# Two pairs of PSUM tiles made into one ring of four, and loads of the second MLP laid between its products

## The chip, the core and the metric

The kernel runs on one core of one Trainium2 chip. Its engines are TensorE (PE, matrix products; PEld is its loading of weights), VectorE (DVE), ScalarE (ACT), GpSimd (POOL) and SyncE (SP, which here only issues DMA transfers). Products are written to PSUM, of which this program uses eight tiles ("banks" here) of 128 x 512 fp32 values; the other engines read them there. The metric is the device time of one launch in microseconds. Lower is better.

## The reference

```python
# x (8, 8, 512, 64), state (8, 8, 32, 64): B, H, S|Ns, D
scores  = x @ state^T / 8;  a  = softmax(scores);   xread = a @ state
scores2 = state @ x^T / 8;  a2 = softmax(scores2);  sread = a2 @ x
t = concat([xread, sread], axis=2)           # per batch and head, 544 rows
t = t.transpose(0, 2, 1, 3).reshape(4352, 512)
h = t @ moe_w_in;   g = max(h, 0) + alpha * min(h, 0);  t = g @ moe_w_out     # 512 -> 2048 -> 512
h = t @ moe2_w_in;  g = h - tanh(h);                    out = g @ moe2_w_out  # 512 -> 2048 -> 512
```

All data are fp32. The kernel carries each fp32 operand as a high and a low part and makes a product in three terms (`TERMS`: high by high, and the two mixed ones).

## The kernel before

**First MLP.** The 4352 tokens are nine blocks: 0 to 7 are the 512 `x` rows of a batch each, the last holds the 256 `state` rows. A *visit* (blk, f) works on one block and one of the 16 slices of 128 columns of the hidden layer:

- `emit_h` (L595) makes the *first product*: 12 matmuls (L605) into a PSUM tile `ps_h`, from the pool `ps_h`, which has two banks.
- `act_a` (L609) has ACT write `t = slope * h` (L612), DVE write `h = max(...)` in place in PSUM (L613), ACT write g's high part (L614); `act_b` (L617) has DVE write g's low part (L618). That last read gives the bank of `ps_h` back.
- `emit_o` (L623) adds the *previous* visit's g times `w_out` to the four accumulators `acc` (L633, 12 matmuls). They hold four banks for a whole block.

**Between the matmuls of the visits** a table of visits and places (`plan`) lays the next batch's attention and the products of its states, in short steps. These take their banks from the pool `ps_a`, two banks, by turns: transposes of x `ps_xt` (L460), scores `ps_s` (L494), transposed scores `ps_e` (L528), the read states `ps_r` (L558), `ps_w` (L583), state products' transposes `ps_st` (L361) and the products of a batch's states with `w_in`, `ps_p` (L410, `project_one`). Each is released by its last reader: `ps_p` by DVE L414 (its low part; ACT L413 writes the high one before), `ps_r` by DVE L568 (`wide`), `ps_xt` by ACT L465, `ps_st` and `ps_e` by ACT and DVE (`e2t` L530 among them). Early in the kernel DVE also splits raw weights into parts (`cm`, L115 to L120). The order of instructions is fixed on every engine; an engine works its own in that order.

**Second MLP.** It runs in five *tasks* (block pairs 0, 1, 2, the state rows B, pair 3) of four *octets* each. An octet (L810) makes 14 products of 6 matmuls (L820, `ps_m`), from the task's prepared x tiles and one *chunk* of combined weights (`ch`, seven parts of 512 KB, `load_chunk` L711). Its results are combined (`c` L826 by ACT and L837 by DVE, `t` L830 and L831) and stored to DRAM as `g` (L808, 256 KB each). A task's raw x, the *pair* `rx`, is four loads of 512 KB (`load_pair`, L722, L726). `bank()` (L798) hands out PSUM banks by turns from all three pools. After the tasks, `unit` (L965) makes the last products (L1001).

All these DMAs are issued by SP in the order of the program, and a store is issued behind the loads that stand before it. At the start of a task SP issues the pair of the next one, and in task 0 also the seven parts of chunk 2, before the task's first store. `octet` calls `between(n)` after its product n; there, short steps of a later preparation are made (`fill.go`).

Of the kernel before, what the change touches and what calls it, by code (L numbers as in the profile page):

```python
# [12 lines left out]
F32 = mybir.dt.float32  # L13
# [6 lines left out]
PSUM = bass.MemoryType.PSUM  # L20
DRAM = bass.MemoryType.DRAM

P = 128
# [12 lines left out]
def attention_and_two_mlps(ctx, tc, x, state, w1_in, w1_out, alpha, w2_in, w2_out, out):  # L36
    nc = tc.nc
    B, H, S, D = x.shape
# [18 lines left out]
    w_outs = tc.alloc_tile_pool(name="w_outs", bufs=NF // FQ)  # L57
    w_ins = tc.alloc_tile_pool(name="w_ins", bufs=NF // FQ, side="right")
    ps_acc = ctx.enter_context(tc.tile_pool(name="ps_acc", bufs=4, space=PSUM))
    ps_h = ctx.enter_context(tc.tile_pool(name="ps_h", bufs=2, space=PSUM))  # L60
    ps_a = ctx.enter_context(tc.tile_pool(name="ps_a", bufs=2, space=PSUM))
    dram = ctx.enter_context(tc.tile_pool(name="dram", bufs=1, space=DRAM))

    blocks = [(b, S) for b in range(B)] + [(B, NSB)]
    y_dram = [dram.tile([NCC, P, n], F32, name=f"y{b}") for b, n in blocks]
# [28 lines left out]
    def w_in(f, part):  # L94
        return WI[f // FQ][:, part].rearrange("p c (f m) -> p c f m", f=FQ)[:, :, f % FQ, :]
# [251 lines left out]
    def lead(b):  # L347
        return b if b % 2 or b == B - 1 else b - 1
# [244 lines left out]


    def emit_h(blk, n, f):  # L595
        ps = ps_h.tile([P, S], F32, tag="h", name="ps_h")
        if 0 < blk < B:
            col = slice(f % FQ * P, (f % FQ + 1) * P)
            pairs = [([PW[blk, f // FQ, g][i][:, col] for i in range(2)], X[0, blk, g]) for g in range(NG)]
        else:  # L600
            w = [WS[f][:, i] if blk else w_in(f, i) for i in range(2)]
            pairs = [([w[i][:, cc, :] for i in range(2)], X[0, blk, cc]) for cc in range(NCC)]
        for k, (w, xt) in enumerate(pairs):
            for m, (i, j) in enumerate(TERMS):
                nc.tensor.matmul(ps[:, :n], lhsT=w[i], rhs=xt[:, j, :n], start=(k == 0 and m == 0),  # L605
                                 stop=(k == len(pairs) - 1 and m == 2))
        return ps[:, :n]
# [94 lines left out]
    slots, small = Slots(), Slots()  # L702
# [8 lines left out]
    def load_chunk(o, i):  # L711

        t = slots.get([P, 2, 2, HW], F32R, f"ch{o}_{i}")
        nc.sync.dma_start(out=t.bitcast(F32), in_=wc_dram[0][o][i].rearrange("j p h c -> p j h c"))
        CH[o, i] = t
# [3 lines left out]

    RX, XT = {}, {}  # L720

    def load_pair(u):  # L722
        for k in range(2):
            for m in range(2):
                t = slots.get([P, 2, S], F32, f"rx{u}_{k}{m}")
                nc.sync.dma_start(out=t, in_=y_dram[2 * u + m][2 * k:2 * k + 2].rearrange("c p n -> p c n"))  # L726
                RX[u, k, m] = t

    def split_to(o, src):
        nc.scalar.copy(o[:, 0], src)  # L730
# [65 lines left out]
    turn = [0]  # L796

    def bank(shape=(P, S)):  # L798

        pool, tag = ((ps_a, "a"), (ps_a, "a"), *[(ps_acc, "acc")] * 4, (ps_h, "h"), (ps_h, "h"))[turn[0] % 8]  # L800
        turn[0] += 1
        return pool.tile(list(shape), F32, tag=tag, name="ps_m")

# [55 lines left out]
    def load_state_block():  # L859
        for k in range(2):  # L860
            XS["r", k] = slots.get([P, 2, NSB], F32, f"xsr{k}")
            nc.sync.dma_start(out=XS["r", k], in_=y_dram[B][2 * k:2 * k + 2].rearrange("c p n -> p c n"))
# [13 lines left out]
    def state_slices(j, between):  # L876


        ps = bank((P, 2, NSB))
        for m, pair in enumerate((((P1, "1"), (P2, "2")), ((P5, "1"), (P4, "d")))):  # L880
            for a, (i, x) in enumerate(pair):
                w = [chunk(j, i, p) for p in range(2)]
                for cc in range(2):
                    for k, (p, q) in enumerate(TERMS):
                        nc.tensor.matmul(ps[:, m], lhsT=w[p][:, cc], rhs=XS[x][:, q, cc],  # L885
                                         start=(a == cc == k == 0), stop=(a == cc == 1 and k == 2))
            between(m)
        t = small.get([P, 2, NSB], F32, f"ts{j}")
        nc.scalar.activation(t, ps, AF.Tanh)
        nc.vector.tensor_tensor(t, ps, t, op=ALU.subtract)  # L890
        for m in range(2):
            store_g(B, m, j, t[:, m])
        small.put(t)
# [4 lines left out]
    def load_weights(i):  # L898
        WP[i] = []
        for jj in range(NJ // 2):  # L900
            t = slots.get([P, 2, 2, HW], F32R, f"wp{i}_{jj}")
            nc.sync.dma_start(out=t.bitcast(F32), in_=wc_dram[1][jj][i].rearrange("r p h c -> p r h c"))
            WP[i].append(t)

    def load_g(blk, k):
        n = blocks[blk][1]
        for jj in range(NJ // 2):
            t = slots.get([P, 2, n], F32, f"gt{blk}_{k}_{jj}")
            nc.sync.dma_start(out=t, in_=g_dram[blk, k, jj].rearrange("r p n -> p r n"))
            GT[blk, k, jj] = t  # L910
# [151 lines left out]
    with tc.manual_schedule():  # L1062
# [5 lines left out]
        a = attention(0, 0)  # L1068
        c = attention(0, 1, spare=True)
# [22 lines left out]
        a = attention(1, 0)  # L1092
# [9 lines left out]
        for b in range(2, B):  # L1102
            for g in range(NG):
                i, f = (0, 0) if b == 2 else (b - 2, 6 + 7 * g) if b == lead(b) else (b - 2, 1 + g)
# [26 lines left out]
        for i, (blk, n) in enumerate(seq):  # L1131
            if i + 1 < B:
                timetable(i, a, attention(i + 1, 1))
                if i + 2 < B:
                    a = attention(i + 2, 0)
# [31 lines left out]
        def open_slots():  # L1167
            for _ in combined:
                pass
            late_pools[0].release()  # L1170
            freed.append(tc.alloc_tile_pool(name="slots_a", bufs=1, side="right", reuse_waits="tile"))
            slots.add(freed[0], "a", 16)
            load_pair(0)
            for i in range(7):
                load_chunk(0, i)
# [12 lines left out]
        for i, f in visits:  # L1188
            blk, n = seq[i]
# [26 lines left out]
        pool = tc.alloc_tile_pool(name="slots_b", bufs=1, reuse_waits="tile")  # L1216
# [6 lines left out]
        for i in range(7):  # L1223
            load_chunk(1, i)
        at_visit = 0
        for k, (u, os) in enumerate(tasks):
            coming = tasks[k + 1][0] if k + 1 < len(tasks) else None
            if coming is None:
                load_weights(P1)
                load_g(0, 0)  # L1230
                load_g(0, 1)
            elif coming == B:
                load_state_block()
                load_pair(3)
            elif u != B:
                load_pair(coming)
            if k == 0:
                for i in range(7):
                    load_chunk(2, i)
            for n_o, o in enumerate(os):  # L1240
                rest = visits[at_visit + 1:]
                following = next((v for v in rest if v > 1), None)

                def used(i):
                    if o not in rest or (o > 1 and following != o):
                        slots.put(CH.pop((o, i)))
                        if o > 1 and following is not None:
                            load_chunk(following, i)

                at_visit += 1  # L1250
                if u == B:
                    for j in (2 * o, 2 * o + 1):
                        state_slices(j, lambda m: fill.go(2))
                    for i in (P1, P2, P5, P4, P6, P3, P7):
                        used(i)
                    continue
                last = n_o == len(os) - 1

                def between(n):
                    if k == 0 and n_o == 0 and n < 5:  # L1260
                        fill.go(3)
                    if coming is None:
                        if n_o == 2 and n == 5:
                            fill.start(prepare_all())
                        if len(ST) < 4:
                            fill.go(1)
                        return
                    if n_o == 1 and n == 0:
                        if coming == B:
                            def both():  # L1270
                                yield from prepare_state_block()
                                yield from prepare_pair(3, 3)
                            fill.start(both())
                        else:
                            fill.start(prepare_pair(coming, coming))
                    if last or n % 2:
                        fill.go(1)

                octet(u, u, (2 * o, 2 * o + 1), between, last, used)
                if coming is None and n_o in (1, 2):  # L1280
                    load_weights((P5, P6)[n_o - 1])
            if u == B:
                for name in "12d":
                    slots.put(XS.pop(name))
            if coming is not None and coming != B:
                fill.finish()
# [40 lines left out]
```

## Time and profile before

| | |
|---|---|
| median of 3 runs | 1509.73 us (1509.43 to 1513.57) |
| the profiled execution | 1510.44 us, span of its work 1508.6 us |
| mean granted TensorE clock | 0.982 |
| PE busy | 1422.1 us, 94% of the span, 8188 matmuls |
| DVE / ACT / POOL busy | 991.6 (66%) / 729.7 (48%) / 532.1 (35%) us |
| 29 to 814 us | first products of the first MLP (L605) and their visits |
| 815 to 1158 us | products of the second MLP's octets (L820) |
| 1158 to 1508 us | its last products (L1001) |

Times in the trace are us from the start of the span. PE is busy nearly all the time, so what counts is its idle gaps, and in which stage another engine sets the pace. A row of a *timeline* gives start, duration, engine, line, operation, tile out<-in, how many instructions it joins, and in brackets the idle time of the engine just before and whose work ended it.

### The profile page before, as it was taken

The numbers are of one execution on the slowest core, as the hardware profiler recorded it, in microseconds if no ns is written. First come the engines' busy times: TensorE is split into PE (matmuls) and PEld (weight loads), VectorE is DVE, ScalarE is ACT, GpSimd is POOL, SyncE is SP. The second block draws the span as 40 slices with busy tenths as digits, with TensorE's granted clock in tenths as the row PEclk, the third lists the DMA queues.
The fourth block names the chain that finished last, engine by engine and source line by source line (L and its number), as shares of the span: only waits on it lengthen the run. The fifth ranks groups of instructions, "written<-read, shape, count | busy, mean of one in ns | idle before, by whom it ended". The sixth has DMA issues, their size and how long they took to land. (4 is left out here: it accounts for less than half of the span.)

```text
span 1508.6 us, 22873 instructions
## 1 busy us (share of the span) xinstructions
PE 1422.1 (94%) x8188; PEld 1192.1 (79%) x8188; DVE 991.6 (66%) x1430; ACT 729.7 (48%) x1322; POOL 532.1 (35%) x414
## 2 busy tenths in 40 slices
PE   5868899999899999999999899999999999999998
PEld 2656687677677677778887787887988999999998
DVE  6879855556577667676345555646347798788874
ACT  3656543444565555555334444545345444444443
POOL 2545400000254444445200222212016486666662
PEclk9998999999999999999999999999999999999999
DMA  5458628795688587749864666272795834444321
GB/s 150 137 163 253 206 80 286 268 300 129 188 213 238 156 247 225 239 158 298 237 209 151 253 202 247 103 272 105 276 346 205 324 133 141 133 141 140 133 85 36
DMA packets 230979, 294.41 MB, mean 195 GB/s; under 512 B 57809, under 2 KB 133585, under 8 KB 229841
## 3 DMA queue, kind: packets, MB, share of 16 engines
q1 hardware_dynamic: 228608, 292.39, 60.2%
q8 instruction: 64, 1.05, 0.3%
q10 hardware_dynamic: 2256, 0.56, 0.2%
q14 instruction: 51, 0.41, 0.1%
HBM read 170.73 MB, written 122.16 MB: 194 GB/s over the span
## 5 line engine op out<-in xcount | busy, mean ns | idle before, releaser
L633 PE MATMUL acc<-g,wo 128*128 128x512 f32 (+1 forms) x1728 | 416.2, 388 | 20.8 <-ACT g L614 11.8
L633 PEld LDWEIGHTS acc<-g,wo 128*128 128x128 f32 x1728 | 312.2, 191 | 104.0 <-ACT g L614 16.6
L1001 PE MATMUL ps_m<-wp,s 128*128 128x256 f32 x2856 | 343.5, 283 | 2.1 <-ACT e L984 2.0
L1001 PEld LDWEIGHTS ps_m<-wp,s 128*128 128x128 f32 x2856 | 342.5, 191 | 3.2 <-ACT e L984 2.2
L820 PE MATMUL ps_m<-x,ch 128*128 128x512 f32 x1344 | 312.7, 394 | 8.6 <-DVE c L837 4.5
L820 PEld LDWEIGHTS ps_m<-x,ch 128*128 128x128 f32 x1344 | 251.7, 188 | 69.0 <-DVE c L837 6.5
L946 DVE TENSOR_TENSOR s<-gt,s 128x512 fp32r<-128x512 f32 (+1 forms) x216 | 220.5, 1072 | 45.4 <-ACT s L962 44.4
L613 DVE SCALAR_TENSOR_TENSOR ps_h<-ps_h,sign,t 128x512 f32<-128x512 f32 (+1 forms) x144 | 104.7, 727 | 144.9 <-ACT t L612 144.4
L614 ACT ACTIVATE g<-ps_h,sign 128x512 fp32r<-128x512 f32 (+1 forms) x144 | 95.8, 666 | 160.5 <-DVE ps_h L613 160.5
L962 ACT CAST s<-gt 128x512 fp32r<-128x512 f32 (+1 forms) x216 | 120.3, 597 | 90.9 <-PE ps_m L1001 37.5
L605 PE MATMUL ps_h<-x,pw 128*128 128x512 f32 x624 | 162.7, 396 | 0.9 <-DMA pw<-pw 0.9
L618 DVE SCALAR_TENSOR_TENSOR g<-ps_h,sign,g 128x512 fp32r<-128x512 f32 (+1 forms) x144 | 102.6, 713 | 62.1 <-ACT g L614 58.9
L612 ACT ACTIVATE t<-ps_h,slope 128x512 f32<-128x512 f32 (+1 forms) x144 | 95.7, 664 | 88.3 <-PE ps_h L605 88.0
L605 PEld LDWEIGHTS ps_h<-x,pw 128*128 128x128 f32 x624 | 114.4, 188 | 26.1 <-issue 1.3
L237 POOL TENSOR_TENSOR c_q<-c_m,c_q 128x512 int32<-128x512 int32 x32 | 42.2, 1319 | 262.3 <-ACT c_q L124 213.0
L831 POOL TENSOR_TENSOR t<-c,t 128x512 f32<-128x512 f32 x32 | 41.7, 1303 | 252.1 <-ACT t L830 239.9
L830 ACT ACTIVATE t<-c 128x512 f32<-128x512 f32 x96 | 60.5, 632 | 123.2 <-DVE c L837 110.3
L837 DVE TENSOR_TENSOR c<-ps_m,c 128x512 f32<-128x512 f32 x96 | 64.7, 685 | 58.9 <-PE ps_m L820 43.2
L264 POOL TENSOR_TENSOR c_o<-c_q,c_o 128x512 fp32r<-128x512 f32 (+1 forms) x48 | 54.4, 1134 | 109.6 <-ACT c_o L262 109.6
L831 DVE TENSOR_TENSOR t<-c,t 128x512 f32<-128x512 f32 x64 | 53.9, 843 | 46.6 <-ACT t L830 46.6
L928 POOL TENSOR_TENSOR s<-gt,gt 128x512 f32<-128x512 f32 (+1 forms) x36 | 53.5, 1492 | 83.2 <-DMA gt<-g 81.5
L167 POOL TENSOR_TENSOR cq<-cm,cq 128x512 int32<-128x512 int32 x32 | 42.0, 1313 | 95.7 <-DVE cm L120 60.5
(138 smaller groups left out, 1663.0 us busy)
## 6 DMA issues: line engine op xcount, KB each, us to landing
g<-t SPq DMA_DIRECT2D x128, 256.0 KB, 2.3
gt<-g SPq DMA_DIRECT2D x64, 512.0 KB, 4.9
wc<-c_o SPq DMA_DIRECT2D x112, 256.0 KB, 3.4
ch<-wc SPq DMA_DIRECT2D x56, 512.0 KB, 7.6
pw<-pw SPq DMA_DIRECT2D x104, 256.0 KB, 5.1
wp<-wc SPq DMA_DIRECT2D x28, 512.0 KB, 7.6
raw<-in_moe_w_in SPq DMA_DIRECT2D x16, 512.0 KB, 4.6
raw<-in_moe_w_out SPq DMA_DIRECT2D x16, 512.0 KB, 4.8
```

Of the source, the lines that this page charges most:

```text
L605: nc.tensor.matmul(ps[:, :n], lhsT=w[i], rhs=xt[:, j, :n], start=(k == 0 and m == 0), stop=(k == len(pairs) - 1 and m == 2))
L612: nc.scalar.mul(t, ph, slope[:, f:f + 1])
L613: nc.vector.scalar_tensor_tensor(ph, ph, sign[:, f:f + 1], t, op0=ALU.mult, op1=ALU.max)
L614: nc.scalar.mul(g[:, 0, :n], ph, sign[:, f:f + 1])
L618: nc.vector.scalar_tensor_tensor(g[:, 1, :n], ph, sign[:, f:f + 1], g[:, 0, :n].bitcast(F32), op0=ALU.mult, op1=ALU.subtract)
L633: nc.tensor.matmul(acc[t][:, :n], lhsT=w[i][:, t * P:(t + 1) * P], rhs=g[:, j, :n], start=(first and k == 0), stop=(last and k == 2))
L820: nc.tensor.matmul(b, lhsT=w[p][:, cc], rhs=XT[key, i][cc][:, q], start=(i not in GOES_ON and cc == k == 0), stop=(cc == 1 and k == 2), sk ...
L831: eng.tensor_tensor(t, h, t, op=ALU.subtract)
L837: nc.vector.tensor_tensor(h, ps[j, i], h, op=ALU.add)
L946: nc.vector.tensor_tensor(made[k - 1][:, 1], src, made[k - 1][:, 0].bitcast(F32), op=ALU.subtract)
L962: nc.scalar.copy(made[k][:, 0], source(blk, i, jj))
L1001: nc.tensor.matmul(dst[:, t * HW:(t + 1) * HW], lhsT=s[:, p, r, t * P:(t + 1) * P], rhs=w[:, q], start=first, stop=(jj == NJ // 2 - 1 and ...
```

## The change

The two pools of two banks become one pool of four, `ps_a`, which serves first products, attention and states' products alike; `bank()` takes four banks of it and then the four of `ps_acc`. `load_pair` gets a part of its own for each load. In the second MLP's tasks 0 and 1 the next pair's four loads, and in task 0 chunk 2's seven loads, are put in a list, and one is taken from it after every odd product of an octet.

```diff
-    ps_h = ctx.enter_context(tc.tile_pool(name="ps_h", bufs=2, space=PSUM))
-    ps_a = ctx.enter_context(tc.tile_pool(name="ps_a", bufs=2, space=PSUM))
+    ps_a = ctx.enter_context(tc.tile_pool(name="ps_a", bufs=4, space=PSUM))
...
     def emit_h(blk, n, f):
-        ps = ps_h.tile([P, S], F32, tag="h", name="ps_h")
+        ps = ps_a.tile([P, S], F32, tag="a", name="ps_h")
...
+    def load_pair_part(u, k, m):
+        t = slots.get([P, 2, S], F32, f"rx{u}_{k}{m}")
+        nc.sync.dma_start(out=t, in_=y_dram[2 * u + m][2 * k:2 * k + 2].rearrange("c p n -> p c n"))
+        RX[u, k, m] = t
...
     def bank(shape=(P, S)):
-        pool, tag = ((ps_a, "a"), (ps_a, "a"), *[(ps_acc, "acc")] * 4, (ps_h, "h"), (ps_h, "h"))[turn[0] % 8]
+        pool, tag = (*[(ps_a, "a")] * 4, *[(ps_acc, "acc")] * 4)[turn[0] % 8]
...
+        loads = deque()
         for k, (u, os) in enumerate(tasks):
...
             elif u != B:
-                load_pair(coming)
+                loads.extend(partial(load_pair_part, coming, h, m) for h in range(2) for m in range(2))
             if k == 0:
-                for i in range(7):
-                    load_chunk(2, i)
+                loads.extend(partial(load_chunk, 2, i) for i in range(7))
...
                 def between(n):
+                    if loads and n % 2:
+                        loads.popleft()()
```

The instructions of PE, DVE, ACT and POOL stay the same and in the same order; what changes there is what they wait for. On PE, at one place of the first MLP (about 82 to 98 us of the trace; names are tiles, and a wait names the engine waited for), it reads so before:

```order
L410 MATMUL ps_p_919<-wi0_342,snp_784 128x512 [waits DVE_49]
L410 MATMUL ps_p_919<-wi0_342,snp_784 128x512 x2
L633 MATMUL acc_518<-g_787,wo1_704 128x512 x3
L633 MATMUL acc_519<-g_787,wo1_704 128x512 x3
L633 MATMUL acc_520<-g_787,wo1_704 128x512 x3
L633 MATMUL acc_521<-g_787,wo1_704 128x512 x3
L410 MATMUL ps_p_939<-wi0_342,snp_784 128x512 [waits DVE_49]
L410 MATMUL ps_p_939<-wi0_342,snp_784 128x512 x2
L460 MATMUL ps_xt_947<-ident_90,xr1_1_405 128x128 [waits DMAHW1_49,DMAHW0_49,DVE_49]
L460 MATMUL ps_xt_947<-ident_90,xr1_1_405 128x128 x3
L605 MATMUL ps_h_966<-x0_0_0_350,wi1_666 128x512 [waits Activation_49]
```

and so in the changed kernel, where these line numbers are one less:

```order
L409 MATMUL ps_p_916<-wi0_339,snp_781 128x512 [waits PE_49]
L409 MATMUL ps_p_916<-wi0_339,snp_781 128x512 x2
L632 MATMUL acc_515<-g_784,wo1_701 128x512 x3
L632 MATMUL acc_516<-g_784,wo1_701 128x512 x3
L632 MATMUL acc_517<-g_784,wo1_701 128x512 x3
L632 MATMUL acc_518<-g_784,wo1_701 128x512 x3
L409 MATMUL ps_p_936<-wi0_339,snp_781 128x512 [waits DVE_49]
L409 MATMUL ps_p_936<-wi0_339,snp_781 128x512 x2
L459 MATMUL ps_xt_944<-ident_87,xr1_1_402 128x128 [waits DMAHW1_49,DMAHW0_49,DVE_49]
L459 MATMUL ps_xt_944<-ident_87,xr1_1_402 128x128 x3
L604 MATMUL ps_h_963<-x0_0_0_347,wi1_663 128x512 [waits DVE_49,Activation_49]
```

The first product `ps_h` of the last row now also waits for DVE: its bank is one of the four, and was the previous first product's, released by L618. The second `ps_p` and `ps_xt` wait on DVE in both, but for banks that were given back earlier: `ps_p` for the bank of the `ps_p` two before it in place of that of `ps_r`, `ps_xt` for that of `ps_r` in place of that of the `ps_p` before it.

On SP, at the start of the second MLP (`rx` the next pair, `ch2` chunk 2, `g` a store of results), it reads so before:

```order
L714 DMA ch1_6_7725<-wc0_1_98 128x2x512
L726 DMA rx1_00_7727<-y2_83 128x2x512
L726 DMA rx1_01_7729<-y3_84 128x2x512
L726 DMA rx1_10_7731<-y2_83 128x2x512
L726 DMA rx1_11_7733<-y3_84 128x2x512
L714 DMA ch2_0_7735<-wc0_2_99 128x2x512
L714 DMA ch2_1_7737<-wc0_2_99 128x2x512
L714 DMA ch2_2_7739<-wc0_2_99 128x2x512
L714 DMA ch2_3_7741<-wc0_2_99 128x2x512
L714 DMA ch2_4_7743<-wc0_2_99 128x2x512
L714 DMA ch2_5_7745<-wc0_2_99 128x2x512
L714 DMA ch2_6_7747<-wc0_2_99 128x2x512
```

and in the changed kernel:

```order
L713 DMA ch1_6_7722<-wc0_1_95 128x2x512
L723 DMA rx1_00_7751<-y2_80 128x2x512
L723 DMA rx1_01_7793<-y3_81 128x2x512
L810 DMA g1_0_0_146<-t0_01_7811 128x512
L723 DMA rx1_10_7815<-y2_80 128x2x512
L810 DMA g1_0_0_146<-t1_01_7832 128x512
L723 DMA rx1_11_7836<-y3_81 128x2x512
L810 DMA g1_1_0_150<-t0_11_7845 128x512
L810 DMA g0_0_0_138<-t0_00_7857 128x512
L713 DMA ch2_0_7861<-wc0_2_96 128x2x512
L810 DMA g1_1_0_150<-t1_11_7870 128x512
L810 DMA g0_0_0_138<-t1_00_7882 128x512
```

The eleven loads, which stood in one row ahead of the first store, now stand between the stores of the first two octets.

## Rows read from the trace of the kernel before

**Rows 1.** Windows by stage: busy time of each engine, granted clock (1 is full), DMA.
```profile
44.00:165.00 121.00, 95.95 (x496) 71.43 (x495) 104.24 (x163) 76.23 (x141) 63.04 (x48) 0.90 0.64 193
165.00:708.00 543.00, 517.74 (x2652) 398.48 (x2651) 346.55 (x593) 275.49 (x498) 159.66 (x153) 0.99 0.70 212
814.00:860.00 46.00, 40.70 (x175) 32.20 (x174) 28.77 (x40) 21.84 (x40) 9.07 (x5) 1.00 0.79 293
```
**Rows 2.** Waits of PE, 44 to 165 us: us in total, times, longest.
```profile
PE ps_xt L460 <- DVE wi L414: 4.1, 1, 4.1
PE ps_p L410 <- DVE wi L414: 3.2, 1, 3.2
PE ps_st L361 <- ACT e2t L530: 2.2, 1, 2.2
```
**Rows 3.** The timeline of PE, 77 to 98 us.
```profile
78.83 3.05 PE L605 MATMUL ps_h<-x,wi 128*128 128x512 f32 x12
92.38 1.11 PE L460 MATMUL ps_xt<-ident,xr 128*128 128x128 f32 x4 [4.13 <-DVE wi L414]
93.14 4.66 PE L605 MATMUL ps_h<-x,wi 128*128 128x512 f32 x12
```
**Rows 4.** The timeline of DVE, 53 to 100 us.
```profile
53.70 0.76 DVE L613 SCALAR_TENSOR_TENSOR ps_h<-ps_h,sign,t 128x512 f32<-128x512 f32 x1 [0.30 <-ACT t L612]
...
62.69 0.76 DVE L613 SCALAR_TENSOR_TENSOR ps_h<-ps_h,sign,t 128x512 f32<-128x512 f32 x1 [0.68 <-ACT t L612]
...
79.29 0.69 DVE L414 TENSOR_TENSOR wi<-ps_p,wi 128x512 fp32r<-128x512 f32 x1 [1.48 <-ACT wi L413]
...
90.98 0.74 DVE L618 SCALAR_TENSOR_TENSOR g<-ps_h,sign,g 128x512 fp32r<-128x512 f32 x1
...
99.49 0.76 DVE L613 SCALAR_TENSOR_TENSOR ps_h<-ps_h,sign,t 128x512 f32<-128x512 f32 x1 [3.88 <-ACT t L612]
```
**Rows 5.** Windows of two stretches with a lowered clock.
```profile
93.00:98.00 5.00, 5.00 (x19) 4.01 (x18) 2.23 (x5) 2.92 (x5) 2.66 (x2) 0.63 0.97 295
295.00:300.00 5.00, 5.00 (x18) 3.93 (x17) 2.90 (x6) 2.13 (x5) 0.00 (x0) 0.69 1.01 395
```
**Rows 6.** Waits of PE, 165 to 815 us.
```profile
PE acc L633 <- ACT g L614: 11.8, 12, 2.9
...
PE ps_p L410 <- DVE pl L414: 3.2, 3, 2.7
PE ps_st L361 <- ACT e2t L530: 2.6, 2, 1.3
...
PE ps_p L410 <- ACT stt L365: 0.4, 1, 0.4
...
PE ps_p L410 <- ACT e2t L530: 0.2, 1, 0.2
```
**Rows 7.** The timeline of PE, 288 to 300 us.
```profile
294.47 1.47 PE L410 MATMUL ps_p<-wi,snp 128*128 128x512 f32 x3 [2.67 <-DVE pl L414]
...
299.64 0.95 PE L410 MATMUL ps_p<-wi,snp 128*128 128x512 f32 x3
```
**Rows 8.** The timeline of DVE, 289 to 297 us.
```profile
295.84 0.75 DVE L618 SCALAR_TENSOR_TENSOR g<-ps_h,sign,g 128x512 fp32r<-128x512 f32 x1
```
**Rows 9.** The timeline of SP's queue, 817 to 866 us.
```profile
824.19 9.15 SPq L714 DMA_DIRECT2D ch<-wc  x7
```
**Rows 10.** DMA issues, 834 to 840 us: KB each, median us to landing.
```profile
g<-t SPq DMA_DIRECT2D x4, 256.0 KB, 9.4
```
**Rows 11.** DMA issues, 848 to 862 us.
```profile
g<-t SPq DMA_DIRECT2D x5, 256.0 KB, 2.0
```
**Rows 12.** The timeline of ACT, 838 to 850 us.
```profile
845.04 1.56 ACT L826 COPY c<-ps_m 128x512 f32<-128x512 f32 x3 [6.59 <-DMA g<-t]
```
**Rows 13.** The timeline of PE, 822 to 860 us.
```profile
826.00 17.10 PE L820 MATMUL ps_m<-x,ch 128*128 128x512 f32 x72 [1.39 <-ACT c L826]
845.68 11.17 PE L820 MATMUL ps_m<-x,ch 128*128 128x512 f32 x48 [2.57 <-ACT c L826]
```

More of the change, by code (lines that the diff above doesn't have):

```diff
@@ L724, in load_pair @@
             for m in range(2):
-                t = slots.get([P, 2, S], F32, f"rx{u}_{k}{m}")
-                nc.sync.dma_start(out=t, in_=y_dram[2 * u + m][2 * k:2 * k + 2].rearrange("c p n -> p c n"))
-                RX[u, k, m] = t
+                load_pair_part(u, k, m)
     def split_to(o, src):
```

## The prediction

> **What bounds the kernel now.** I read the windows by stage first: they give each engine's busy time, so the busiest engine of a stage and what it leaves idle. From 165 to 708 us PE works 517.74 of 543 us; there PE is the bound, and a wait of PE that goes is time won, unless another wait takes it. From 44 to 165 us it is not: PE works 95.95 of 121 us and DVE 104.24, since DVE splits raw weights beside its other work. There a wait of PE only counts as far as DVE too gets on earlier. From 814 to 860 us PE works 40.70 of 46 us, with the DMA engines 0.79 busy [rows 1].
>
> Then I listed what PE waits for. Before 165 us the three longest waits that the change touches are 4.1, 3.2 and 2.2 us, each for the *last reader of an older tile*: `ps_xt` cannot want DVE's `wi` (L414), which reads `ps_p`; it wants the bank that `ps_p` held [rows 2]. That is how a shortage of banks looks: the releaser is no producer of the operands. The two banks of the attention's pool go round quickly, while those of the first products stand free for long. After 165 us the same pattern is 3.2 us for L414 and 2.6 us for `e2t`, and smaller lines down to 0.2; the largest wait there, 11.8 us for ACT's g (L614), is a wait for an operand, and no bank changes it [rows 6].
>
> **The change part by part: the ring, 44 to 165 us (term A).** No instruction of PE, DVE, ACT or POOL is added or moved; only the bank of a tile changes. I took each PSUM tile's first write and the last read of the tile that held its new bank, both at their times in the trace. In every wait of 0.5 us or more the new bank was free at least 1.0 us before the wait began. What counts is DVE: its idle spots 0.30 at 53.70, 0.68 at 62.69 and 1.48 at 79.29, together 2.5, end at an ACT step that stands behind PE products held up by a bank, so DVE's later work moves up by as much [rows 4]. With that, g's L618, which ends at 90.98 + 0.74 = 91.72 [rows 4], ends at about 89.2. This is the bank that the first product at 93.14 takes in the new order; in place of 93.14, where it now stands behind `ps_xt` and its 4.13 us wait [rows 3], it can start at 89.2, 3.9 us earlier. [...] The DVE step behind it, L613 at 99.49, had waited 3.88 us [rows 4]. So it comes 3.9 us earlier if the clock falls all the same (PE still stands for some 3 us before that product, now for L618, since the steps ahead of it come earlier too), and 3.9 + 1.6 = 5.5 if not. I take 4.5, nearer to the low end, since PE's clock fell in such a gap. The upper bound is 5.5. The lower bound is 0: behind 99 us, DVE and the loads and stores of weights work nearly without a pause, and could keep all of it.
>
> **The ring, 165 to 814 us (term B).** PE is the bound here. The waits that go are 2.6 (`ps_st`, two), 0.5 of the 3.2 for L414 (two short ones), 0.4 and four lines of 0.2 to 0.3, of which I count 0.5, since two of them get a bank that is as late as now: 2.6 + 0.5 + 0.4 + 0.5 = 4.0 [rows 6]. The long one is `ps_p` at 294.47, 2.67 us [rows 7]. It goes, and with it the clock of 0.69 in the 5 us behind it, worth 5 x 0.31 = 1.5 us, as far as no new gap comes [rows 5]. But then the `ps_p` that stands at 299.64 would start 2.67 + 1.5 earlier, at 295.4, and its new bank is that of a first product, which DVE's L618 gives back at 295.84 + 0.75 = 296.6 [rows 7, 8]: that is late next, 1.2 us. Net 2.67 + 1.5 - 1.2 = 3.0. Queued behind that new wait are the rest of PE's products alone. B = 4.0 + 3.0 = 7.0. Upper bound 8.2, without the new wait. Lower bound 3: PE that arrives earlier at an accumulator's products waits there for ACT's g, as it does twelve times already [rows 6], and can lose a part of each gain.
>
> **The loads in the second MLP (term C).** SP issues the next pair's four loads and chunk 2's seven, 11 x 512 KB, before the first store; the seven take 9.15 us to issue, till 833.3, and the first store stands behind them [rows 9]. Stores issued from 834 on land after 9.4 us, against 2.0 us for those from 848 on [rows 10, 11]. ACT's copy of a product (L826) stands 6.59 us for such a store, whose tile it needs, until 845.04 [rows 12], and PE 2.57 us for ACT, until 845.68 [rows 13]. With the loads between the products, a store has no more than one or two loads of 512 KB ahead of it. I take its landing as 2 to 4 us, between rows 11 and 10 and nearer to 11; then ACT's wait goes, and PE's 2.57 with it. The wait of 1.39 at 826.00, for the same line of ACT before any store is due [rows 13], stays. C = 2.6; upper bound 2.57 + 1.39 = 4.0, lower 0. The moved loads cost nothing if they land before their use. Each pair part and chunk part now goes out at every second product, 2 x 6 x 17.10 / 72 = 2.85 us apart [rows 13]; eleven take 31 us, till about 847, and chunk 2 is first needed in the third octet, 168 matmuls after the first, at 0.24 us each and with the gaps about 857. Some 10 us of slack; if that cover were gone, the price is a landing, up to 9.4 us.
>
> **Sum.** 4.5 + 7.0 + 2.6 = 14.1 us. The profiled execution took 1510.44 us, 0.7 above the median of 1509.73: 1510.4 - 14.1 = 1496.3; as a median of runs 1495.6, and I forecast between the two, 1496.0 us.
>
> [...] PE stands for banks for 9.5 us in the three longest waits of the first stretch [rows 2]. [...]
>
> **The rivals.**
> *The early gain is lost* (A = 0). For it: from 44 to 165 us DVE is 86% busy and the DMA engines 0.64 [rows 1], and what DVE gains can stand again before a weight's load. Against it: the loads are issued as buffers come free, so they move with DVE. Time: 1510.4 - 9.6 = 1500.8.
> *The loads only change places* (C = 0). The stores now stand behind loads one by one, and ACT or the combination of products waits as long in smaller pieces. For it: 0.79 of DMA in that window is needed either way [rows 1]. Against it: landings of 9.4 us behind those loads and of 2.0 us without them [rows 10, 11]. Time: 1510.4 - 11.5 = 1498.9.
> *The ring relieves nothing* (A and B = 0): waits for operands, 11.8 us for ACT's g alone, take the place of those for banks [rows 6]. Against it: `ps_st` and `ps_p` at 294.47 are in stretches where PE has the most work. Time 1507.8, no difference that counts.
> *Slower.* Until now a first product had a bank of its own pair, free since the first product before last; in the ring a `ps_p` or a `ps_h` can take the bank of the visit just before, and PE then stands for DVE's L618, as worked out at 299.64. There are 9 x 16 = 144 visits. If that wait of 1.2 us came at one visit in six, 24 x 1.2 = 29 us would be lost against 14 won: 1510.4 + 15 = 1525. It decides from (14.1 + 4.5) / 1.2 = 16 such places on. Against it: by the working above on the trace of before, 13 tiles whose bank changes have less than 1 us to spare, and only one has none, 0.1 us late; a delay to DVE would have to hit all.
>
> **How the numbers follow.** The forecast (all three terms in their bounds) 0.56; the early gain lost 0.21; loads only change places 0.13; ring relieves nothing 0.07; slower 0.03. The terms at their upper bounds give 1510.4 - 17.7 = 1492.7, less the 0.7 of the median 1492.0; the first two rivals end at 1500.8; with A lost and B at its lower bound it is 1510.4 - 5.6 = 1504.8. I set 1491.5 to 1503.5, which leaves out the last two cases and a part of the second. A difference of 0.3%, 4.5 us, is about what a measurement of this kernel can tell from none: faster than 1505.2 are the first three cases, 0.90 less a share of 0.02 with low terms: 0.88; the same 0.09; slower 0.03.
>
> **What would show it.** In the trace after: no waits of PE for L414 or `e2t` L530 of the lengths in [rows 2, 6]; the first product of 93.14 at about 89, that of 299.64's `ps_p` with a wait for L618 of about 1 us; windows 4 to 5 us shorter before 165 and 7 shorter from there to 814; the clock of 0.69 gone; stores near 835 landing in under 5 us and PE's 2.57 gone. The forecast is wrong if DVE's idle time before 165 us turns up again behind a DMA, if the waits for ACT's g grow by what the bank waits lose, or if the third octet begins with a wait for chunk 2.

## The result and the profile after

The changed kernel takes 1493.82 us (median of 4 runs, 1491.91 to 1494.18), the one before beside it 1510.13 (4 runs, 1509.43 to 1513.57): the ratio is 0.9885, with a 95% interval of 0.9868 to 0.9902, 16.3 us by the medians. The forecast was 1496.0, in a range of 1491.5 to 1503.5. The profiled execution took 1493.87 us with a span of 1492.1, 16.5 less than before.

The windows of the changed kernel, in the columns of [rows 1]; the third is the stretch that holds the same work as 814 to 860 before:

```profile
44.00:165.00 121.00, 100.30 (x515) 75.10 (x513) 109.19 (x168) 77.56 (x143) 66.19 (x50) 0.92 0.65 196
165.00:708.00 543.00, 520.57 (x2713) 405.60 (x2712) 349.14 (x599) 279.67 (x507) 164.95 (x160) 0.99 0.72 218
801.00:844.00 43.00, 40.32 (x174) 32.26 (x173) 28.80 (x40) 22.14 (x40) 9.06 (x5) 1.00 0.89 314
```

In the first stretch both PE and DVE do more in the same time: 515 matmuls in place of 496, DVE 109.19 us of 121 in place of 104.24. The same work at the start of the second MLP fits into 43 us in place of 46.

PE's waits from 20 to 165 us, in the columns of [rows 2]:

```profile
PE ps_h L604 <- DVE g L617: 5.3, 3, 2.9
...
PE ps_r L557 <- ACT e2t L529: 3.9, 1, 3.9
...
PE ps_e L527 <- DVE g L617: 1.9, 1, 1.9
...
PE ps_h L604 <- DVE wi L413: 1.0, 1, 1.0
```

The waits of 4.1, 3.2 and 2.2 us of [rows 2] are gone. New ones stand for g's L617, the last reader of a first product, at four places, and one for L413, the last reader of a `ps_p`; `e2t` at `ps_r` is an operand and stood there before. From 165 to 810 us, against [rows 6]:

```profile
PE acc L632 <- ACT g L613: 11.5, 12, 2.9
PE acc L632 <- DVE g L617: 6.0, 14, 1.2
PE ps_p L409 <- DVE g L617: 1.8, 1, 1.8
...
PE ps_p L409 <- ACT stt L364: 0.4, 1, 0.4
```

All 3.2 us for `pl` (L414) and 2.6 for `e2t` are gone, the waits for ACT's g did not grow (11.8 before), and one new wait of 1.8 us came. The two places that were named, on PE's timeline, against [rows 3, 7]:

```profile
85.47 0.60 PE L459 MATMUL ps_xt<-ident,xr 128*128 128x128 f32 x4
89.02 4.58 PE L604 MATMUL ps_h<-x,wi 128*128 128x512 f32 x12 [2.95 <-DVE g L617]
...
284.87 0.86 PE L409 MATMUL ps_p<-wi,snp 128*128 128x512 f32 x3
...
290.56 1.44 PE L409 MATMUL ps_p<-wi,snp 128*128 128x512 f32 x3 [1.84 <-DVE g L617]
291.80 2.68 PE L604 MATMUL ps_h<-x,pw 128*128 128x512 f32 x6
294.31 0.86 PE L409 MATMUL ps_p<-wi,snp 128*128 128x512 f32 x3
```

and DVE there, against [rows 4, 8]:

```profile
87.38 0.83 DVE L340 TENSOR_TENSOR x<-at,x 128x512 fp32r<-128x512 f32 x1 [1.74 <-ACT x L339]
88.13 0.74 DVE L617 SCALAR_TENSOR_TENSOR g<-ps_h,sign,g 128x512 fp32r<-128x512 f32 x1
...
289.75 0.75 DVE L617 SCALAR_TENSOR_TENSOR g<-ps_h,sign,g 128x512 fp32r<-128x512 f32 x1
```

`ps_xt` no longer waits, and the first product stands behind L617, which ends at 88.13 + 0.74 = 88.87. The granted clock of both places, in the columns of [rows 5]:

```profile
89.00:94.00 5.00, 4.99 (x17) 3.90 (x17) 4.24 (x7) 2.15 (x4) 2.61 (x3) 0.66 0.79 248
291.00:296.00 5.00, 5.00 (x17) 3.96 (x16) 2.51 (x7) 2.11 (x5) 0.00 (x0) 0.68 1.05 400
```

It fell at both again, to 0.66 and 0.68, after PE had stood for 2.95 and 1.84 us. At the start of the second MLP, the stores issued from 818 to 826 us against [rows 10], and PE against [rows 13]:

```profile
g<-t SPq DMA_DIRECT2D x4, 256.0 KB, 3.6
```

```profile
812.89 27.97 PE L822 MATMUL ps_m<-x,ch 128*128 128x512 f32 x120 [1.40 <-ACT c L828]
842.14 8.18 PE L822 MATMUL ps_m<-x,ch 128*128 128x512 f32 x34 [1.28 <-DVE c L839]
```

A store lands after 3.6 us in place of 9.4, and 120 matmuls run without a gap where 2.57 us stood. That the second comes of the first is not shown by this: the stores also go out earlier (see the experiments on which loads). From 800 to 870 us PE waits for no part of chunk 2.

**Where the time came from.** PE's instructions are the same in the same order in all kernels of this study (a *lead* is how much earlier one starts than in the trace of before), so each one's start can be set against its start in the trace of before. The table gives the lead so found, in us, one trace for each kernel (their edits are below): at the `ps_p` of 164.59 in the trace of before; what is gained from there to 800, and from 840 to 858; and at the last products.

| kernel | lead at 165 | 165 to 800 | 840 to 858 | at the end |
|---|---|---|---|---|
| changed kernel | 4.3 | 8.8 | 2.9 | 16.4 |
| the same again | 5.6 | 11.2 | 2.9 | 17.9 |
| ring, chunk 2 moved | 5.2 | 7.8 | 2.9 | 16.5 |
| ring alone | 8.0 | 7.3 | -1.3 | 14.2 |
| ring until 165 | 8.0 | 1.0 | 0.2 | 9.6 |
| ring from 165 on | 0.9 | 9.9 | -1.5 | 8.0 |
| loads alone | 1.2 | 1.2 | 2.9 | 4.1 |
| pair's loads alone | 0.6 | 1.1 | 0.9 | 2.8 |
| chunk 2's loads alone | 0.7 | 2.2 | 2.9 | 5.9 |

The five with the ring in the first stretch lead by 6.2 on average, the four with pairs by 0.9: the ring is worth 5.4 there (forecast A = 4.5). From 165 to 800 the five with the ring gain 9.0 and the four with pairs 1.4: 7.6 (B = 7.0). The moved loads are worth 2.9 (C = 2.6). Together 15.9. What kernels without a change gain there, 0.6 to 1.2 in the first and 1.0 to 2.2 in the second stretch, is how far the one trace of before lay behind others of the same instructions.

### The profile page after: what moved, and what is told of

It is laid out like the page before. It is cut to its first block, busy times and chain, and to the rows that moved or that the text cites. A ratio compares the mean times of both kernels' runs of the same rounds, so it can differ in the third digit from the quotient of the medians.

```text
span 1492.1 us, 22871 instructions
## 1 busy us (share of the span) xinstructions
PE 1416.3 (95%) x8188; PEld 1190.3 (80%) x8188; DVE 990.1 (66%) x1430; ACT 729.4 (49%) x1322; POOL 531.7 (36%) x414
## 4 chain that ended last, share of the span: by engine, by line
PE 65%; DVE 8%; DMA 6%; ACT 5%; issue 3%; POOL 1%; SPq 1%; DVEq 0%; ACTq 0%; POOLq 0%
PE ps_m L1003 20%; PE ps_m L822 17%; PE acc L632 14%; PE ps_h L604 8%; PE ps_p L409 2%; DVE ps_h L612 2%; DVE g L617 2%; PE ps_m L887 2%; ACT g L613 1%; DMA c_raw<-in_moe_w_in 1%; ACT t L611 1%; DMA g<-t 1%; DVE c L839 1%; DMA wp<-wc 1%; DMA gt<-g 1%
## 5 line engine op out<-in xcount | busy, mean ns | idle before, releaser
L948 DVE TENSOR_TENSOR s<-gt,s 128x512 fp32r<-128x512 f32 (+1 forms) x216 | 217.4, 1058 | 44.5 <-ACT s L964 43.4
L617 DVE SCALAR_TENSOR_TENSOR g<-ps_h,sign,g 128x512 fp32r<-128x512 f32 (+1 forms) x144 | 102.6, 713 | 61.8 <-ACT g L613 59.1
```

The source lines that it names most:

```text
L617: nc.vector.scalar_tensor_tensor(g[:, 1, :n], ph, sign[:, f:f + 1], g[:, 0, :n].bitcast(F32), op0=ALU.mult, op1=ALU.subtract)
L948: nc.vector.tensor_tensor(made[k - 1][:, 1], src, made[k - 1][:, 0].bitcast(F32), op=ALU.subtract)
```

## The experiments

**The parts alone.** First the ring with the loads as before, and the loads with the pools as before:

```diff
 ring_alone, against the changed kernel:
-                loads.extend(partial(load_pair_part, coming, h, m) for h in range(2) for m in range(2))
+                load_pair(coming)
...
-                loads.extend(partial(load_chunk, 2, i) for i in range(7))
+                for i in range(7):
+                    load_chunk(2, i)
```

```diff
 loads_alone, against the changed kernel:
-    ps_a = ctx.enter_context(tc.tile_pool(name="ps_a", bufs=4, space=PSUM))
+    ps_h = ctx.enter_context(tc.tile_pool(name="ps_h", bufs=2, space=PSUM))
+    ps_a = ctx.enter_context(tc.tile_pool(name="ps_a", bufs=2, space=PSUM))
...
-        ps = ps_a.tile([P, S], F32, tag="a", name="ps_h")
+        ps = ps_h.tile([P, S], F32, tag="h", name="ps_h")
```

> The ring of four banks alone, with the second MLP's loads where they stood before. Theory (the gain is made of separate waits, for banks in the first MLP and for stores behind loads in the second): at the last products of the first MLP the changed kernel was 13.1 us ahead of the one before, so this one should be 13.1 faster, about 1497.0 us, and its trace should show the wait of PE of about 2.6 us near 833 us again, behind a store that lands late. Rival (the ring's gain needs the moved loads, or is given back in the second MLP, whose loads now start earlier against the first MLP's last stores): less than 10 us faster, 1500 or more.

> The moved loads alone, with the two pairs of banks of before. Theory: only PE's wait of 2.57 us for the store and what the changed kernel gained between there and 860 us, 2.9 in all, so about 1507.2 us. Rival (the moved loads gain only because the ring comes earlier to that place): nothing, 1510. First MLP: shift of 0 within 0.5 us against the kernel before.

The ring alone took 1496.86 us against 1508.87 (17 runs of before beside these four kernels): ratio 0.9924 (0.9906 to 0.9942), 12.0 faster. Its lead at 814 us is 15.3, and the wait for the store is back, on PE's and ACT's timelines:

```profile
830.10 12.81 PE L822 MATMUL ps_m<-x,ch 128*128 128x512 f32 x48 [2.27 <-ACT c L828]
```

```profile
829.46 1.56 ACT L828 COPY c<-ps_m 128x512 f32<-128x512 f32 x3 [6.30 <-DMA g<-t]
```

The loads alone took 1505.20, ratio 0.9974 (0.9960 to 0.9987), 3.7 faster. In its first MLP, where nothing is changed, its trace was 2.4 us ahead by 814 us, not within the 0.5 expected: so much do traces of the same instructions differ. The parts are separate and add up: 12.0 + 3.7 = 15.7 against 16.3 for both. The rivals of both expectations fall.

**The ring in one stretch alone.** A table gives each tile in turn its bank, once as the ring hands them out and once as the two pairs did, and changes from one to the other at the `ps_p` of 164.6 us:

```diff
-    ps_a = ctx.enter_context(tc.tile_pool(name="ps_a", bufs=4, space=PSUM))
+    ps_ring = ctx.enter_context(tc.tile_pool(name="ps_ring", bufs=1, space=PSUM))
+    ring_banks = iter(
...
+    class Ring:
+        def tile(self, shape, dtype, tag, name):
+            return ps_ring.tile(shape, dtype, tag="r" + next(ring_banks), name=name)
+
+    ps_a = Ring()
```

> The ring's banks up to the ps_p at 164.6 us, the two pairs' banks from there on, loads as before. Theory: what the changed kernel was ahead at 165 us, 4.3 us, stays to the end: about 1505.8. Rival (the early gain is given back, since DVE and the loads of weights set the pace there or later): within 1 us of before.

> The two pairs' banks up to 164.6 us, the ring's from there on, loads as before. Theory by waits for banks alone: 7.0 us faster, 1503.1. Theory by waits and by the stretches at the lower clock that went with them: 8.8, as in the trace of the changed kernel between 165 and 814 us, about 1501.3, with no lowered clock near 730 us. Both say that early and late parts add up to the ring alone; the rival of a coupling (only with the early gain do the places after 165 us move) says less than 5 us.

The early ring took 1501.75 us, ratio 0.9959 (0.9945 to 0.9974), the late one 1502.74, ratio 0.9958 (0.9943 to 0.9973): 7.1 and 6.1 us faster, 13.2 together against 12.0 for the ring alone. The 7.1 is above the 4.3 that the first trace of the changed kernel gave to expect; its own trace led by 8.0 at 165 us. So the early gain stays to the end, and the rival that gives it back falls; nor is there a coupling. For the late one, 6.1 is nearer to 7.0, the theory of waits alone, but the interval (4.1 to 8.6) holds both values.

**Which loads.** Each kind of load alone is laid between the products, with the pools of before (and, for the third, chunk 2's alone beside the ring):

```diff
 pair_alone, against loads_alone:
-                loads.extend(partial(load_chunk, 2, i) for i in range(7))
+                for i in range(7):
+                    load_chunk(2, i)
...
 chunk_alone against loads_alone, and ring_chunk against the changed kernel:
-                loads.extend(partial(load_pair_part, coming, h, m) for h in range(2) for m in range(2))
+                load_pair(coming)
```

> Banks and chunk 2's loads as before; only the pairs' loads of tasks 0 and 1 are laid between products. Theory (a backlog of bytes: a store lands when what stands ahead of it has been moved): 4 x 512 KB less stand ahead of the first stores, at some 390 GB/s 5.4 us, so the wait of ACT for a store, 6.59 us before, shrinks to about 1.2 and PE's 2.57 us to less than 1. Rival (what counts is that no load at all stands ahead of a store in the queue): ACT's wait stays above 4 us and PE's above 1.5.

> Banks and the pairs' loads as before; only chunk 2's seven loads are laid between products. Theory of the backlog: 7 x 512 KB less, 9.4 us, so neither ACT nor PE waits there any more (PE's 2.57 gone). Rival of the order in the queue: PE still waits more than 1.5 us there, since four loads stand ahead of the stores.

With the pair's loads alone (one run, 1507.42 us) ACT still stands for a store, on its timeline:

```profile
840.92 1.07 ACT L829 COPY c<-ps_m 128x512 f32<-128x512 f32 x2 [4.18 <-DMA g<-t]
842.83 0.58 ACT L829 COPY c<-ps_m 128x512 f32<-128x512 f32 x1 [0.83 <-DMA g<-t]
```

The wait of PE for ACT, 2.57 us before, is gone, but PE stands 0.94 and 1.58 us for DVE at 852 and 856, where 1.34 stood: 0.9 us are left of 2.9. ACT's 4.18 is the rival's, so the bytes ahead do not tell a store's landing by themselves: the first store went out at 829.84 us, 4.5 earlier than before, but still behind chunk 2's seven loads, and stores issued from 834 to 840 us took 8.5 us to land. With chunk 2's loads alone (one run, 1504.37) neither ACT nor PE waits for a store there, and the whole 2.9 is won, as the backlog had it.

That is not because a store takes less time to land. SP's queue before and with chunk 2's loads alone, and the landing of the stores that the latter issues from 825 to 834 us, against [rows 10]:

```profile
834.30 29.30 SPq L808 DMA_DIRECT2D g<-t  x16
```

```profile
825.76 0.33 SPq L811 DMA_DIRECT2D g<-t  x1
```

```profile
g<-t SPq DMA_DIRECT2D x4, 256.0 KB, 9.2
```

These stores take 9.2 us, nearly the 9.4 of before, but the first goes out 8.5 us earlier, of which 2.8 are the lead of that trace: 5.7 us that it no longer stands in SP's queue behind the issue of chunk 2's loads. An earlier issue alone thus does away with both waits; a landing of 3.6 us, which the changed kernel has beside it, is not needed.

> The ring, and chunk 2's seven loads alone laid between products; the pairs' loads as before. Theory (chunk 2's bytes ahead of the first stores were the whole cause of PE's 2.57 us): the same time as the changed kernel, within 2 us, and no wait of PE for a store near 830 us. Rival: 1 to 2 us slower with a part of that wait back.

The ring with chunk 2's loads moved took 1493.18 us (ratio 0.9891, 0.9870 to 0.9912), beside 1492.04 for the changed kernel (0.9887, 0.9868 to 0.9907): the same. Its stores issued from 815 to 833 us took 8.3 us to land, and still PE's only waits there are the 1.4 at ACT's line and the 1.3 at DVE's of the changed kernel:

```profile
813.03 28.00 PE L822 MATMUL ps_m<-x,ch 128*128 128x512 f32 x120 [1.38 <-ACT c L828]
```

Moving the pair's loads as well adds nothing that shows in the time.

**One bank for first products.** Pools of one and three in place of two and two:

```diff
-    ps_h = ctx.enter_context(tc.tile_pool(name="ps_h", bufs=2, space=PSUM))
-    ps_a = ctx.enter_context(tc.tile_pool(name="ps_a", bufs=2, space=PSUM))
+    ps_h = ctx.enter_context(tc.tile_pool(name="ps_h", bufs=1, space=PSUM))
+    ps_a = ctx.enter_context(tc.tile_pool(name="ps_a", bufs=3, space=PSUM))
```

> As before, but three banks for the attention and one for first products (bank() by threes and one). It forces what the rival Slower feared: each first product takes the bank of the one just before, and PE stands until DVE's L618 has read it. Theory: in the trace of before that read ends after the next first product's start at 100 of 143 places, by 136 us in all; waits that come first shift later ones, so half of it to all: 60 to 136 us slower, 1570 to 1645. If this is so, the ring is faster only because its banks are handed out to whoever comes next in the order of their release. Rival (first products seldom wait, other work covers it): less than 30 us slower.

It took 1556.62 us, ratio 1.0306 (1.0284 to 1.0328), 47.6 slower. PE's waits over the whole span begin with

```profile
PE ps_h L605 <- DVE g L618: 74.2, 73, 5.9
```

1.0 us each, at 73 places. The price lies between the two theories, below the first one's 60: such waits take the place of those for ACT's and DVE's g, 11.8 + 8.2 us before, over the whole span, of which 0.2 are left. So the mechanism of the rival Slower is real; the ring meets it at a handful of places only.

**What is late next.** One entry of the table of visits puts x's low part behind g's, and beside it the changed kernel was run again:

```diff
-                        s3x=(4, "gap"), s3b=(4, "late"), s4=(4, "end"), s4m=(4, "end"), s4t=(4, "end"), s4b=(5, "gap"),
+                        s3x=(4, "gap"), s3b=(4, "late"), s4=(4, "end"), s4m=(4, "end"), s4t=(4, "end"), s4b=(5, "mid"),
```

> The changed kernel with one edit in its table of visits: the low part of x (L340) of the step s4b in visit 5 of block 0 stands behind g's L617 in place of ahead of it. It tries what was said to be late next: in the changed kernel the first product at 89.02 us waits 2.95 us for L617, which stands behind L340, for which DVE waits 1.74 us for ACT. Theory (that release sets the time there): L617 ends 2 us earlier, PE's wait falls from 2.95 to about 0.7, and with the clock that fell there up to 1.5 more: 2 to 4 us earlier than the changed kernel at 100 us and still at 165 us, so about 1491. Rival (DVE's or the loads' amount of work sets the pace until 165 us): the shift is gone by 165 us and the time is that of the changed kernel, 1493.8.

> The changed kernel once more, beside the two below on one chip. What is open: it was 4.3 us ahead at 165 us in its first trace, and two kernels with the same instructions up to there were 8.0 ahead. If the clock made that difference (it fell behind the 2.95 us wait at 89 us in the first trace and not behind those of 2.1 and 1.9 in the others), this trace has either a wait of over 2.5 us with a first product of about 4.6 us behind it and is 4 to 5 us ahead, or a shorter wait with one of 3.05 and is 7 to 8 ahead. Time 1492 to 1494.

> x (L340) behind g's L617, beside the changed kernel on one chip. Theory that DVE sets the pace till 165 us: the same time as the changed kernel, within 2 us, since the lead at 100 us is gone by 165. Theory that the release by L617 does: 3 us faster than the changed kernel.

The first trace with this edit, PE and then DVE:

```profile
84.70 0.60 PE L459 MATMUL ps_xt<-ident,xr 128*128 128x128 f32 x4
85.05 3.05 PE L604 MATMUL ps_h<-x,wi 128*128 128x512 f32 x12
```

```profile
84.20 0.75 DVE L617 SCALAR_TENSOR_TENSOR g<-ps_h,sign,g 128x512 fp32r<-128x512 f32 x1 [0.17 <-ACT g L613]
85.75 0.69 DVE L413 TENSOR_TENSOR wi<-ps_p,wi 128x512 fp32r<-128x512 f32 x1 [0.80 <-ACT wi L412]
86.36 1.54 DVE L340 TENSOR_TENSOR x<-at,x 128x512 fp32r<-128x512 f32 x1
```

PE's wait for L617 is gone, and the lead over before is 8.8 us at 100, against 7.1 in the ring alone, whose start was as early; at 165 it is 8.4 against 8.0. In its second trace 0.35 us of the wait are left, and the lead is 7.8 at both:

```profile
85.96 3.08 PE L604 MATMUL ps_h<-x,wi 128*128 128x512 f32 x12 [0.35 <-DVE g L617]
```

The times are 1490.67 in the first comparison (ratio 0.9876, 0.9861 to 0.9891) and, beside the changed kernel's 1492.04, 1490.73 (0.9885, 0.9867 to 0.9903): no difference that can be told. Which theory holds is left open. Against the rival (DVE's amount of work) stands that the lead at 100 us is still there at 165, and that 8.4 and 7.8 are about 3 us more than the 4.3 and 5.6 of the changed kernel, as the theory of the release had it; against that theory stands that the ring alone and the early ring reach 8.0 at 165 without this edit. A version that beats the changed kernel has not been shown.

The changed kernel again had the shorter of the two waits at 89 us, and the clock stayed up (PE's timeline, then the window):

```profile
88.79 3.04 PE L604 MATMUL ps_h<-x,wi 128*128 128x512 f32 x12 [1.50 <-DVE g L617]
```

```profile
89.00:94.00 5.00, 5.00 (x22) 2.99 (x21) 4.50 (x8) 3.05 (x6) 2.62 (x3) 1.00 0.78 239
```

Its lead is 6.0 at 100 us and 5.6 at 165, against 4.2 and 4.3 in the first trace: this product took 1.5 us less, as expected in kind, but the lead is less than the 7 to 8 named. The 8.0 of the ring alone has another part: it was 1.8 us ahead by 44 us, before the first tile that had waited for a bank. The early ring was not (it had lost that lead again by 44 us), and why it too reached 8.0 is open.

## Why the prediction was right

- **The mechanism** was right in kind in all three terms, as the parts alone and the sum of 15.9 show: waits for banks went, and waits for late stores went. None of the four rivals came true; that A and B are not nothing is shown by the 12.0 us of the ring alone. The sum agrees better than its pieces; in B that is in part luck.
- **A = 4.5, measured 4.3 in the changed kernel's trace, 5.4 over the traces.** The step "ends at about 89.2" for L617's release was 88.87, the first product at 89.02 for 89.2, and the choice "nearer to the low end, since PE's clock fell in such a gap" held in this trace (0.66); in the second trace the clock stayed up (1.00), which the upper bound of 5.5 stood for. The 1.6 us in that bound is 4.66 - 3.05, the two products of twelve matmuls in [rows 3]; the same product took 4.58 us in this trace and 3.04 in the second. The lower bound of 0 was too careful: DVE kept the lead, because it was DVE's own idle time that went: its waits between 44 and 165 us add up to 14.8 us before and 9.6 after.
- **B = 7.0, measured 8.8 in this trace, above the stated bound of 8.2, and 7.6 over the traces.** Two terms were mis-sized and the base was off. In us of the trace of before, the lead of the changed kernel grows by 2.5 from 165 to the `ps_p` at 294.47, by 0.7 from there to 305 (forecast: net 3.0), by 3.2 on to 380, by 0.2 on to 712 and by 2.3 on to 735. So the shorter waits, counted as 4.0, gave 5.7: at the two `ps_st` of 1.30 and 1.33 the lead rises by 1.5 each, more than their idle time. The 2.3 is the base: the sum took waits only, and counted a lowered clock (0.69) at one place. In the trace of before a gap of 1.78 us for ACT's g at 726.55 was followed by a lowered clock (first row, before, 0.79); the same place in the changed kernel, 1.30 us, was not (second row):

```profile
726.00:734.00 8.00, 7.31 (x46) 7.12 (x47) 2.44 (x5) 2.68 (x6) 1.17 (x2) 0.79 1.04 320
```

```profile
713.00:721.00 8.00, 6.42 (x49) 5.85 (x48) 2.93 (x6) 3.06 (x8) 2.00 (x2) 1.00 1.07 344
```

  By an estimate from the first row that is 8 x 0.21 = 1.7 us, and no doing of the ring: loads alone, with the pairs of before, gained 2.2 from 712 to 735 too. Without it B is 8.8 - 2.3 = 6.5 in this trace.
- **The place at 294.47** was right in kind and wrong in size: the wait of 2.67 went and a new one for L617 came, at the tile named; it was 1.84 for 1.2, and the clock's 1.5 us did not stay won, since it fell again behind the new gap (0.68 for 0.69). "As far as no new gap comes" was the right proviso, and the net 3.0 ignored it. In this trace the lead grows from 6.8 us before that tile to 299.64 - 290.56 = 9.1 at the `ps_p` that waits, but the products behind it run slowly now, as six did for 2.68 us (291.80 above) where they had taken 1.54:

```profile
300.44 1.54 PE L605 MATMUL ps_h<-x,pw 128*128 128x512 f32 x6
301.82 0.87 PE L410 MATMUL ps_p<-wi,snp 128*128 128x512 f32 x3
```

  At the next `ps_p` the lead is 301.82 - 294.31 = 7.5: 0.7 won in all. Over the traces the five kernels with the ring gain 1.3 on average from 294.47 to 305, and the four with pairs 1.5, whose waits there were 1.4 to 2.0 us for 2.67: the largest single term of B gave nothing that shows, and the ring's gain lies in the shorter waits ahead of this place (3.2 us more than with the pairs) and behind it up to 380 us (3.1 more).
- **C = 2.6, measured 2.9.** Both waits went, and the landing taken as 2 to 4 us was 3.6. But the moved loads did not all matter: chunk 2's carry it all, and they do it by letting the stores go out earlier, with landings of 9.2 us; the prediction had named that the first store stands behind their issue, and reckoned with the landing alone.
- **Slower** asked for 16 new waits of 1.2 us for L617. There are five in the first MLP, 9.0 us in all (5.3 + 1.9 + 1.8), and two for other last readers (1.0 and 0.3 us), where the working on the trace of before found one tile late besides the first product near 89 us. They stand in place of some 21 us of waits for banks, added up from the timelines of before (13.9 until 165 us and 7.0 behind).

**A part of it is clock.** In the first trace PE is busy 1416.3 us, 5.8 less than before, with the same matmuls and a mean granted clock of 0.986 in place of 0.982: so 10.7 us of the 16.5 are idle time gone, and 5.8 are the same matmuls in less time. In the second trace of the same kernel PE is busy 1419.1 us at 0.983, and that part is 3.0 of 18.0: a third in one execution, a sixth in the other.

The lowered stretches shown here follow gaps of 1.78 to 4.13 us, but not every gap has one behind it: 2.57 us at 845.68 before were followed by full clock (1.00, first row), while 2.27 at 830.10 in the ring alone were not (0.83, second row):

```profile
845.00:849.00 4.00, 3.32 (x15) 2.75 (x16) 0.69 (x1) 3.20 (x7) 0.00 (x0) 1.00 0.64 245
```

```profile
830.00:840.00 10.00, 9.90 (x36) 8.00 (x37) 4.94 (x7) 4.89 (x10) 0.00 (x0) 0.83 0.36 139
```

The second cost 10 x 0.17 = 1.7 us, by an estimate like the one above; with the 0.3 us by which the wait is shorter that makes about the -1.3 of the table. What decides between them is left open.

## What to carry to other kernels

A wait of a producer for the last reader of an *older* tile is a wait for a buffer, as were the 4.1, 3.2 and 2.2 us of [rows 2] that went with the ring; give such tiles one common pool, if in the order of the program the banks come free before they are wanted, and look which reader is last then, since a step ahead of it in its queue is part of its price (PE's wait for L617 at the first product near 89 us was 2.95 and 1.50 us in the changed kernel, with L340 ahead of L617; with L340 behind it none and 0.35). Take the time of the bound engine, not the waits, as what can be won: in the stretch that DVE bounded, about 5 us came back for 13.9 us of PE's waits, and DVE's own waits fell by 5.2. Loads that are not wanted soon belong behind the stores that somebody waits for, and here chunk 2's seven, the larger part, were enough for the whole 2.9 us. Where a place has gained, follow it on until the clock behind it is back: the gain of a wait can be lost again in slower products, as at 291.80, where six took 2.68 us at a clock of 0.68 in place of 1.54.

## What was not expected of the hardware

One execution of the same instructions differs from the next by more than small edits move: leads at 165 us of 4.3 and 5.6 for the same kernel, and runs of the kernel before from 1504.2 to 1514.1 us (17 runs). Part of that is the clock, which in the windows shown here fell after gaps of 1.78 to 4.13 us (to 0.63 to 0.83) and stayed at 1.00 after gaps of 1.30 to 2.57, each fall worth some 1.5 us (an estimate from the windows and products above): from one trace of before, a term can be read no closer than that.
